# Batch row 0 of a gated linear attention prepared in three tiles of 128 rows, with its first pieces loaded through ScalarE's queue

## The chip, the core and the metric

The kernel runs on one core of a Trainium2 chip. The metric is the device time of one execution in microseconds. The core has five engines with queues of their own: TensorE (PE; its weight loads are PEld in the profile), VectorE (DVE), ScalarE (ACT), GpSimd (POOL) and SyncE (SP), and 16 DMA engines that serve the DMA queues of SP, ScalarE and GpSimd. Within a queue instructions run in the order in which the program was written; engines wait for one another through semaphores.

## The reference

A gated linear attention over 4 batch rows of 8 heads, 768 positions and 48 features, and behind it two layers of experts. Only the attention is touched:

```python
def _attn_ref(q, k, v, alpha):
    B, H, S, D = q.shape            # 4, 8, 768, 48
    state = np.zeros((B, H, D, D))
    for t in range(S):
        state = alpha[:, :, t, :, None] * state + np.einsum('bhd,bhe->bhde', k[:, :, t], v[:, :, t])
        y[:, :, t] = np.einsum('bhd,bhde->bhe', q[:, :, t], state)
```

Its output, as 3072 tokens of 384 features, goes through a layer that sends each token to the one of eight experts with the largest logit (`relu(x @ w1[e]) @ w2[e]`, times the gate's weight), and then through a dense layer `silu(x @ w_in) @ w_out`.

## The kernel before

The attention works on 16 pairs of heads, four to a batch row: pair p is pair p % 4 of batch row p // 4. In a pair, one head's 48 features lie on partitions 0 to 47 and the other's on 64 to 111; partitions 48 to 63 are a gap, and a pair fills 112 rows. A sequence is cut in six chunks of 128 positions.

Before PE can use a pair, its alpha, q and k have to be prepared: a running product of alpha (`f0`, line 535, a scan on DVE, with a reciprocal at line 538), q times that product (`scaled_q`, line 547; on GpSimd, but on DVE for tile 0), the decay of each chunk (`decay`, line 542, ScalarE), a scan from the end (`f1`, line 553, DVE) and k times that (`f2`, line 558, DVE). This runs on tiles T. In batch row 0 a tile is a pair: four tiles of 112 rows. In the batch rows 1 to 3 the fourth pair rides along with the other three: its 96 rows lie in six blocks of 16 in the gaps and behind the ends of three tiles, which so have 128 rows (`ASIDE`). When the three are prepared, six DMAs of 16 rows, issued by GpSimd, collect the fourth pair (`gather_last`, line 520). The prepared tiles are `Es[0]` to `Es[4]`, taken in turn and called E_133 to E_137 in listings; the collected pair is `Es[5]`, E_138. The profile calls them all E.

The loop over p from 0 to 16 (a step) does pair p's scores (`scores`, line 580, PE), transposes of k (`ks_transpose`, 568), the chunk updates (`updates`, 613 and 620) and the state scan (`states`, 630 on DVE, 647 on ScalarE), and beside them the output of pair p - 1 (`from_states`, 658, and `within`, 670 and 673). The masks on the scores are DVE's (586); for the first half of pairs 1 to 4 ScalarE copies and GpSimd masks (599 and 600). The steps of the preparation are hung into the loop by the table `work`: with place(T) = (b, j) and p = 4b + j, the first scan, q's multiply and the decay of tile T come in step p - 2, the reverse scan at the end of step p - 2, k's multiply at the head of step p - 1, and the loads at the start of step p - 3. Tiles 0 to 2 are loaded ahead of the loop. v comes in four buffers, three steps ahead (line 448). Small matmuls on zeros (`warm`, line 508) fill PE in the first steps. At step 2 GpSimd also makes constants.

Everything is issued in the order in which it is written (`manual_schedule`). All loads are SP's, one `dma_start` at a time, and eight such DMAs share eight semaphores in turn: an issue waits until the DMA that used the same one before has landed. All score matmuls write one pair of PSUM banks, so pair p + 1's scores wait for the masks of pair p.

## Time and profile before

| | |
|---|---|
| median of 3 runs | 794.62 us (793.44 to 795.41) |
| the profiled execution | 795.29 us |
| its span | 793.6 us |
| mean granted clock of TensorE | 0.991 |
| PE busy | 768.1 us, 97% |
| DVE busy | 478.9 us, 60% |
| DMA traffic | 80.54 MB, mean 101 GB/s |

The span runs from the first to the last instruction; the execution's own time has 1.7 us more around it. The attention lies in the first 160 us, the experts behind it. Busy time is a share of an average: DVE is at nine tenths in the first stretches of the page and at three or four behind 400 us.

### The profile page before, as it was taken

The page shows a single profiled execution, that of the slowest core. Times are in us where ns is not written, and L with a number is a line of the kernel's source. Part 1 is how long each engine was busy: PE and PEld are TensorE (multiplying, and loading weights), DVE is VectorE, ACT ScalarE, POOL GpSimd, SP SyncE. Part 2 cuts the span into 40 slices and gives each one's busy share as a digit, 9 for nine tenths or more (in the row PEclk, how much of TensorE's full clock was granted, in tenths as well). Part 3 has the DMA queues.
Part 4 walks back from the last instruction along what each step waited for, and adds up shares of the span by engine and source line. Part 5 has one row for each costly group of instructions (what it writes and reads, how often), then busy time and mean ns, then how long its engine had stood idle before and what let it go on. Part 6 is the DMA issues. An engine that isn't in the chain of part 4 may idle for free.

```text
span 793.6 us, 13367 instructions
## 1 busy us (share of the span) xinstructions
PE 768.1 (97%) x5104; PEld 701.0 (88%) x5104; DVE 478.9 (60%) x821; ACT 360.8 (45%) x685; POOL 156.5 (20%) x198
## 2 busy tenths in 40 slices
PE   8999998989999999999999999999999999999995
PEld 6878787889899999999999999999999998999985
DVE  8999975747787887788788433433443343333332
ACT  2656564425444455556544324453544444333322
POOL 4764321230332231311121200020020001002002
PEclk9999999999999999999999999999999999999998
DMA  9788883524554555555210110031022001001001
GB/s 241 212 197 223 217 251 96 172 80 124 172 170 145 183 193 160 189 179 164 94 63 18 38 55 18 0 93 36 1 75 52 19 1 40 2 0 41 1 1 44
DMA packets 41642, 80.54 MB, mean 101 GB/s; under 512 B 5640, under 2 KB 19863, under 8 KB 41568
## 3 DMA queue, kind: packets, MB, share of 16 engines
q1 hardware_dynamic: 37568, 67.56, 29.1%
q0 software_dynamic: 4000, 12.03, 5.1%
q8 instruction: 42, 0.69, 0.4%
q14 instruction: 32, 0.26, 0.1%
HBM read 68.03 MB, written 9.44 MB: 98 GB/s over the span
## 4 chain that ended last, share of the span: by engine, by line
issue 42%; PE 40%; DMA 5%; DVE 4%; POOL 4%; SPq 2%; ACT 2%; POOLq 0%; DVEq 0%; ACTq 0%
PE hp L1197 17%; PE both L1226 9%; PE yb L1226 4%; POOL out_dram L1415 3%; PE both L1393 1%; PE ob L1393 1%; SPq L439 1%; DMA E<-in_q_dram 1%; DMA E<-in_k_dram 1%; PE Yp L658 1%; DMA v__342<-in_v_dram 1%; PE xt L356 1%; PE Yp L673 1%; PE Ap L580 1%; DVE Pf L535 1%
## 5 line engine op out<-in xcount | busy, mean ns | idle before, releaser
L1197 PE MATMUL hp<-xh,wl 128*128 128x512 f32 (+9 forms) x504 | 184.5, 369 | 0.8 <-DVE wl L332 0.8
L1197 PE MATMUL hp<-xh,wh 128*128 128x512 f32 (+9 forms) x504 | 184.5, 369 | 0.0
L1371 DVE TENSOR_TENSOR sg<-hp,sg 128x512 f32<-128x512 f32 (+1 forms) x97 | 66.5, 686 | 157.6 <-ACT sg L1370 153.2
L1197 PE MATMUL hp<-xl,wh 128*128 128x512 f32 (+9 forms) x504 | 130.7, 367 | 0.0
L1370 ACT ACTIVATE sg<-hp 128x512 f32<-128x512 f32 (+1 forms) x97 | 57.5, 593 | 154.8 <-PE hp L1197 149.4
L1197 PEld LDWEIGHTS hp<-xh,wl 128*128 128x128 f32 x504 | 95.3, 189 | 10.1 <-DVE wl L332 0.9
L1197 PEld LDWEIGHTS hp<-xh,wh 128*128 128x128 f32 x504 | 95.1, 189 | 9.9 <-issue 0.4
L1197 PEld LDWEIGHTS hp<-xl,wh 128*128 128x128 f32 x504 | 91.9, 189 | 13.4
L1381 DVE TENSOR_TENSOR hl<-sg,hh 128x512 fp32r<-128x512 f32 x94 | 65.1, 692 | 61.1 <-PE ob L1393 40.5
L1380 ACT CAST hh<-sg 128x512 fp32r<-128x512 f32 x94 | 58.3, 620 | 70.3 <-DVE sg L1371 70.3
L1206 ACT ACTIVATE hh<-hp 128x192 fp32r<-128x192 f32 (+8 forms) x72 | 34.5, 479 | 117.6 <-PE hp L1197 113.4
L1415 POOL DMA_INDIRECT out_dram<-o,sidx x24 | 24.2, 1008 | 322.3 <-ACT o L1413 317.8
L1124 POOL TENSOR_TENSOR wl<-dx,wh 128x384 fp32r<-128x384 f32 x32 | 39.1, 1221 | 194.9 <-ACT wh L1121 191.3
L332 DVE TENSOR_TENSOR wl<-raw,wh 128x768 fp32r<-128x768 f32 x64 | 62.1, 971 | 11.1 <-ACT wh L331 9.9
L1393 PE MATMUL both<-wh,hh 128*128 128x384 f32 x188 | 64.1, 341 | 0.0
L1393 PE MATMUL both<-wh,hl 128*128 128x384 f32 x188 | 64.0, 341 | 0.0
L1208 DVE SCALAR_TENSOR_TENSOR hl<-hp,hh 128x192 fp32r<-128x192 f32 (+8 forms) x72 | 38.9, 540 | 41.2 <-ACT hh L1206 39.9
L1393 PE MATMUL both<-wl,hh 128*128 128x384 f32 x188 | 63.5, 338 | 0.0
L1393 PE MATMUL ob<-wh,hh 128*128 128x384 f32 x188 | 62.8, 334 | 0.0
L1393 PE MATMUL ob<-wl,hh 128*128 128x384 f32 x188 | 62.8, 334 | 0.0
L1393 PE MATMUL ob<-wh,hl 128*128 128x384 f32 x188 | 62.8, 334 | 0.0
L331 ACT CAST wh<-raw 128x768 fp32r<-128x768 f32 x64 | 52.9, 828 | 0.0
(363 smaller groups left out, 1482.2 us busy)
## 6 DMA issues: line engine op xcount, KB each, us to landing
raw<-in_wt_dram SPq DMA_DIRECT2D x64, 384.0 KB, 3.1
raw<-in_w_dram SPq DMA_DIRECT2D x32, 384.0 KB, 3.0
raw<-in_alpha_dram SPq DMA_DIRECT2D x16, 336.0 KB, 3.5
x_d<-xr SPq DMA_DIRECT2D x24, 192.0 KB, 1.9
E<-in_q_dram SPq DMA_DIRECT2D x18, 144.0 KB, 3.9
E<-in_k_dram SPq DMA_DIRECT2D x18, 144.0 KB, 2.8
E<-E POOLq DMA_DIRECT2D x18, 114.0 KB, 5.3
E<-in_q_dram SPq DMA_DIRECT2D x4, 336.0 KB, 9.3
```

The source lines that it names most:

```text
L331: nc.scalar.copy(hi, raw[t])
L332: eng.tensor_tensor(lo, raw.pop(t), hi.bitcast(F32), op=ALU.subtract)
L1124: nc.gpsimd.tensor_tensor(r["lo"], r["x"], r["hi"].bitcast(F32), op=ALU.subtract)
L1197: nc.tensor.matmul(hp, lhsT=a[:, kc * 128 : (kc + 1) * 128], rhs=x[:, kc, c0:c1], start=(i == 0), stop=(i == 8))
L1208: nc.vector.scalar_tensor_tensor(hl[:, :n], in0=hp, scalar=0.0, in1=hh[:, :n].bitcast(F32), op0=ALU.max, op1=ALU.subtract)
L1226: nc.tensor.matmul(yb[dc][:, c0:c1], lhsT=a[:, c : c + 128], rhs=b_[:, : c1 - c0], start=(f == 0 and i == 0), stop=(f == NF - 1 and i == 2),)
L1370: nc.scalar.activation(sg[:, z], hp[:, z], AF.Sigmoid)
L1371: nc.vector.tensor_tensor(sg[:, z], hp[:, z], sg[:, z], op=ALU.mult)
L1380: nc.scalar.copy(hh[:, z], sg[:, z])
L1381: nc.vector.tensor_tensor(hl[:, z], sg[:, z], hh[:, z].bitcast(F32), op=ALU.subtract)
L1393: nc.tensor.matmul(yb[tt], lhsT=a[:, tt * 128 : (tt + 1) * 128], rhs=b_[:, 384:768], start=(f == 0 and i == 0), stop=(f == NF2 - 1 and i = ...
L1415: sc = nc.gpsimd.indirect_dma_start(out=out, out_offset=bass.IndirectOffsetOnAxis(ap=sidx[:, i : i + 1], axis=0), in_=ob, in_offset=None,)
```

## The change

Batch row 0 is prepared as the others are: three tiles of 128 rows, with its fourth pair in their spare rows, and `gather_last(0)` in step 1 collects it. There are 12 tiles instead of 13. A tile's load is four DMAs for each of alpha, q and k, where batch row 0 had one: two of 48 rows and two of 16. The pieces of 16 now go first; those of tile 0 are issued by ScalarE's queue, all others by SP. Tile 0's alpha is still loaded in two halves of its columns, which makes four pieces of 48 rows. On DVE the reverse scan of tile 0 now stands ahead of its multiply by q.

```diff
--- before.py
+++ after.py
@@ -393,7 +393,7 @@
 
 
         ASIDE = (((0, 16), (0, 32)), ((1, 0), (1, 16)), ((1, 32), (0, 0)))
-        NTL = 4 + 3 * (B - 1)
+        NTL = 3 * B
         NE = 5
 
 
@@ -401,10 +401,7 @@
         tl = {}
 
         def place(T):
-            if T < 4:
-                return 0, T
-            b, j = divmod(T - 4, 3)
-            return b + 1, j
+            return divmod(T, 3)
 
         def parts(e):
             return dict(
@@ -429,18 +426,15 @@
             for x in what:
                 src, t = load_to(T, x)
                 n = src.shape[2]
-                z = src[4 * b + j]
-                if b:
-                    z = [(0, z[0:D]), (64, z[64:PA])]
-                    for i, (h, d) in enumerate(ASIDE[j]):
-                        s0 = 64 * h + d
-                        z.append((64 * i + D, src[4 * b + 3][s0 : s0 + 16]))
-                    for r0, y in z:
-                        nc.sync.dma_start(t[r0 : r0 + y.shape[0]], y)
-                else:
-
-                    for c0, c1 in ((0, SP // 2), (SP // 2, n)) if x == "a" and T == 0 else ((0, n),):
-                        nc.sync.dma_start(t[0:PA, c0:c1], z[:, c0:c1])
+                z = [(64 * h, src[4 * b + j][64 * h : 64 * h + D]) for h in range(2)]
+                for i, (h, d) in enumerate(ASIDE[j]):
+                    s0 = 64 * h + d
+                    z.append((64 * i + D, src[4 * b + 3][s0 : s0 + 16]))
+                for r0, y in z[2:]:
+                    (nc.sync if T else nc.scalar).dma_start(t[r0 : r0 + 16], y)
+                for c0, c1 in ((0, SP // 2), (SP // 2, n)) if x == "a" and T == 0 else ((0, n),):
+                    for r0, y in z[:2]:
+                        nc.sync.dma_start(t[r0 : r0 + D, c0:c1], y[:, c0:c1])
 
         def load_v(p):
             if p < NP:
@@ -517,17 +511,17 @@
             for j in range(3):
                 for i, (h, d) in enumerate(ASIDE[j]):
                     s0 = 64 * h + d
-                    nc.gpsimd.dma_start(Es[NE][s0 : s0 + 16], Es[(3 * b + 1 + j) % NE][64 * i + D : 64 * i + 64])
+                    nc.gpsimd.dma_start(Es[NE][s0 : s0 + 16], Es[(3 * b + j) % NE][64 * i + D : 64 * i + 64])
 
         def begin(p):
             b, j = divmod(p, 4)
-            e = Es[p if not b else NE if j == 3 else (3 * b + 1 + j) % NE]
+            e = Es[NE if j == 3 else (3 * b + j) % NE]
             st.setdefault(p, {}).update(parts(e))
 
         def prep(T):
             s = tl[T]
             i = T % 2
-            n = PA if T < 4 else 128
+            n = 128
 
             def f0():
                 s["Pf"] = wk.tile([128, SP], F32, tag="Pf", name="Pf", bufs=3)
@@ -1002,7 +996,7 @@
             for T, i in work.get((p, place), []):
                 f(T, i)
 
-        for i in range(5):
+        for i in (P_SCAN, DECAY, R_SCAN, Q_SCALE, K_SCALE):
             f(0, i)
         for i in (P_SCAN, Q_SCALE, DECAY):
             f(1, i)
@@ -1024,7 +1018,7 @@
                 ks_transpose(p, 0, 3)
                 if beside_scans(p, 0):
                     mask_aside(p, 0)
-            if p % 4 == 1 and 1 < p < NP:
+            if p % 4 == 1 and p < NP:
                 gather_last(p // 4)
             prepare(p, "scan")
             aside(p, "F1")
```

The order of the instructions is that of the code. On GpSimd, this stood ahead of the constants before (E_134 to E_137 are the tiles 1 to 4, Pf the scan's result, Am the masked scores; line 547 is q's multiply, line 600 the mask):

```order
L547 TENSOR_TENSOR E_2_135<-E_2_135,Pf_278 112x768
L600 AFFINE_SELECT Am_364<-Am_364 128x768
L547 TENSOR_TENSOR E_3_136<-E_3_136,Pf_374 112x768
L600 AFFINE_SELECT Am_458<-Am_458 128x768
L547 TENSOR_TENSOR E_4_137<-E_4_137,Pf_468 128x768
L478 MEMSET bm_89 112x1
```

And this stands there now (E_138 is the collected pair; lines are six lower):

```order
L541 TENSOR_TENSOR E_2_135<-E_2_135,Pf_302 128x768
L594 AFFINE_SELECT Am_388<-Am_388 128x768
L514 DMA E_5_138<-E_0_133 16x1824 x2
L514 DMA E_5_138<-E_1_134 16x1824 x2
L514 DMA E_5_138<-E_2_135 16x1824 x2
L594 AFFINE_SELECT Am_481<-Am_481 128x768
L541 TENSOR_TENSOR E_3_136<-E_3_136,Pf_490 128x768
L472 MEMSET bm_89 112x1
```

The multiply of pair 3's own tile has gone, the six DMAs stand between the masks of pair 1 and pair 2, and tile 3, which is pair 4's now, comes ahead of the constants, as pair 4's did.

On DVE, steps 1 and 2 before (So is the state scan, Rv the reverse scan, mask the mask's multiply):

```order
L558 TENSOR_TENSOR E_2_135<-E_2_135,Rv_340 112x768
L535 SCALAR_TENSOR_TENSOR Pf_374<-a__254,Z1_158 112x774
L538 RECIPROCAL D1_1_162<-Pf_374 112x6
L586 TENSOR_TENSOR Am_400<-Ap_393,mask_165 128x768
L630 SCALAR_TENSOR_TENSOR So_424<-U_179,E_1_134 112x288
L553 SCALAR_TENSOR_TENSOR Rv_431<-a__254,D1_1_162 112x774
L558 TENSOR_TENSOR E_3_136<-E_3_136,Rv_431 112x768
L535 SCALAR_TENSOR_TENSOR Pf_468<-a__344,Z1_158 128x774
L538 RECIPROCAL D1_0_161<-Pf_468 128x6
L586 TENSOR_TENSOR Am_521<-Ap_514,mask_165 128x768
L630 SCALAR_TENSOR_TENSOR So_545<-U_179,E_2_135 112x288
```

And now:

```order
L552 TENSOR_TENSOR E_2_135<-E_2_135,Rv_364 128x768
L580 TENSOR_TENSOR Am_425<-Ap_418,mask_193 128x768
L624 SCALAR_TENSOR_TENSOR So_449<-U_207,E_1_134 112x288
L529 SCALAR_TENSOR_TENSOR Pf_490<-a__368,Z1_186 128x774
L532 RECIPROCAL D1_1_190<-Pf_490 128x6
L580 TENSOR_TENSOR Am_543<-Ap_536,mask_193 128x768
L624 SCALAR_TENSOR_TENSOR So_567<-U_207,E_2_135 112x288
```

A scan and a reciprocal have left step 1, and the reverse scan and k's multiply between the two state scans have gone with them; the rest keeps its order.

On PE, pair 3's first scores read the collected pair, and their waits are now these (DMASW0 to DMASW5 are the six DMAs of GpSimd):

```order
L574 MATMUL Ap_593<-E_5_138 128x128 [waits DMASW1_49,DMASW5_49,DMASW0_49,DVE_49]
L574 MATMUL Ap_593<-E_5_138 128x128 [waits DMASW4_49,DMASW3_49,DMASW2_49]
L574 MATMUL Ap_593<-E_5_138 128x128 x4
L562 MATMUL Tp_602<-ident_78,E_5_138 128x112 x3
L502 LDWEIGHTS wz_76
```

The matmuls themselves stand where they stood; what they wait for has moved from a tile of SP's loads to the six DMAs.

## Rows read from the trace of the kernel before

**Rows 1.** The page, part 1: busy us (share of the span) and instructions.

```profile
PE 768.1 (97%) x5104; PEld 701.0 (88%) x5104; DVE 478.9 (60%) x821; ACT 360.8 (45%) x685; POOL 156.5 (20%) x198
```

**Rows 2.** Windows: stretch, its length, busy us by engine, PEclk, DMA share, GB/s.

```profile
9.60:18.40 8.80, 6.62 (x79) 5.33 (x79) 8.63 (x10) 1.92 (x4) 4.77 (x4) 1.00 1.06 262
...
25.00:31.50 6.50, 6.42 (x92) 5.34 (x89) 6.43 (x7) 4.12 (x8) 4.06 (x3) 1.00 0.58 166
...
31.50:38.00 6.50, 6.35 (x91) 5.33 (x89) 6.43 (x7) 4.03 (x8) 6.04 (x25) 1.00 0.83 230
...
164.00:793.00 629.00, 620.71 (x3273) 574.72 (x3272) 344.52 (x600) 278.59 (x516) 90.54 (x102) 0.99 0.25 76
```

**Rows 3.** Timeline of PE: start us, length us, engine, line, operation [idle before].

```profile
25.15 0.94 PE L580 MATMUL Ap<-E 48*128 48x128 f32 x12
...
31.58 0.94 PE L580 MATMUL Ap<-E 48*128 48x128 f32 x12
...
33.90 0.41 PE L568 MATMUL Tp<-ident,E 112*128 112x112 f32 x2 [0.15 <-ACT kst L571]
...
38.11 0.94 PE L580 MATMUL Ap<-E 48*128 48x128 f32 x12
...
45.79 1.03 PE L580 MATMUL Ap<-E 48*128 48x128 f32 x12 [1.38 <-POOL Am L600]
```

**Rows 4.** Timeline of DVE: tile 3's work, then a stretched scan and a mask.

```profile
21.64 1.76 DVE L535 TENSOR_TENSOR_SCAN Pf<-a__254,Z 112x774 f32<-112x774 f32 x1
...
25.04 2.25 DVE L553 TENSOR_TENSOR_SCAN Rv<-a__254,D 112x774 f32<-112x774 f32 x1
...
27.32 0.96 DVE L558 TENSOR_TENSOR E<-E,Rv 112x768 f32<-112x768 f32 x1
...
41.42 3.20 DVE L535 TENSOR_TENSOR_SCAN Pf<-a__558,Z 128x774 f32<-128x774 f32 x1
...
44.76 0.93 DVE L586 TENSOR_TENSOR Am<-Ap,mask 128x768 f32<-128x768 f32 x1
```

**Rows 5.** Timeline of GpSimd (POOL): two operations, then the first gather's six DMA issues.

```profile
21.66 2.40 POOL L600 TENSOR_SCALAR_AFFINE_SELECT Am<-Am 128x768 f32<-128x768 f32 x1 [2.56 <-ACT Am L599]
...
40.66 2.33 POOL L547 TENSOR_TENSOR E<-E,Pf 128x768 f32<-128x768 f32 x1
...
46.83 2.24 POOL L520 DMA_DIRECT2D E<-E  x4
...
50.88 0.96 POOL L520 DMA_DIRECT2D E<-E  x2 [1.82 <-DMA E<-in_q_dram]
```

**Rows 6.** Line 520's own view, its 18 gather DMAs: last line of it.

```profile
DMA to landing us min/median/max: 4.1/5.3/7.9
```

**Rows 7.** Timeline of DVE, the start of the kernel.

```profile
3.40 1.82 DVE L535 TENSOR_TENSOR_SCAN Pf<-a__139,Z 112x387 f32<-112x387 f32 x2 [1.01 <-DMA a__139<-in_alpha_dram]
...
6.00 0.96 DVE L547 TENSOR_TENSOR E<-E,Pf 112x768 f32<-112x768 f32 x1 [0.48 <-DMA E<-in_q_dram]
...
9.55 1.76 DVE L535 TENSOR_TENSOR_SCAN Pf<-a__144,Z 112x774 f32<-112x774 f32 x1
```

**Rows 8.** Timeline of SP's queue: the first DMA issues.

```profile
0.81 0.86 SPq L443 DMA_DIRECT2D a__139<-in_alpha_dram  x2
1.73 0.42 SPq L443 DMA_DIRECT2D E<-in_q_dram  x1
```

**Rows 9.** The page, part 6: DMA issues, count, KB each, median us to landing.

```profile
E<-in_q_dram SPq DMA_DIRECT2D x18, 144.0 KB, 3.9
E<-in_k_dram SPq DMA_DIRECT2D x18, 144.0 KB, 2.8
```

**Rows 10.** Timeline of PE at a wait, and windows of the stretches behind it.

```profile
130.53 0.69 PE L658 MATMUL Yp<-E,Sb 112*112 112x128 f32 x4 [2.42 <-ACT xb L690]
...
130.00:133.40 3.40, 2.87 (x22) 2.62 (x24) 1.78 (x2) 2.32 (x5) 0.00 (x0) 0.69 0.02 5
...
133.40:136.80 3.40, 3.40 (x38) 2.48 (x37) 1.43 (x4) 1.18 (x3) 0.00 (x0) 0.81 0.72 231
```

## The prediction

> **What bounds the kernel now.** I read the page first: PE is busy 97% of the span, DVE 60% [rows 1]. By stretches, everything from 164 us on is PE alone (620.71 of 629.00 us busy) [rows 2], and that work is not touched. What the attention gives or takes ahead of 164 us therefore reaches the end one for one, unless it moves something that waits on a clock of its own. So the question is what sets the pace in the first 46 us, where the change lies. A "step" p is one round of the loop, counted from the first score matmul (line 580) of pair p.
>
> The stretches show two engines close to full: in 9.6 to 18.4 us DVE (8.63 of 8.80 us, PE 6.62), and in the steps 2 and 3 both (PE 6.42 and 6.35 of 6.50 us, DVE 6.43 in each) [rows 2]. The timeline of PE settles which one a saving has to reach: pair 2's scores start at 25.15, pair 3's at 31.58, pair 4's at 38.11, with no idle time written beside these starts and 0.15 us in between at 33.90. The steps last 6.43 and 6.53 us, and PE fills them. PE's first real wait is ahead of pair 5's scores at 45.79, 1.38 us [rows 3]. The row puts it down to a GpSimd mask, but DVE's mask multiply, which started at 44.76 and took 0.93, ends at 45.69 [rows 4] on the score banks that these matmuls write: PE waits there for DVE.
>
> **The change, part by part.**
>
> *DVE loses one tile.* Pair 3 no longer has a tile of its own. Gone are a scan (1.76 us at 21.64), a reverse scan (2.25 at 25.04) and a multiply (0.96 at 27.32) [rows 4], with a reciprocal of 0.1 to 0.2: some 5.1 us. GpSimd loses one multiply of about 1.6 us, ScalarE one small activation; neither ends a wait there. As the order shows, the DVE work goes from steps 1 and 2. PE has no idle time there that DVE ends, so of the 5.1 us only what PE waits for later can be had: the 1.38 us at 45.79 and the 0.15 at 33.90 [rows 3]. Credit: 1.53 us. Its cover is DVE being early at step 4. DVE must not lose that lead again to GpSimd: the scan at 41.42 took 3.20 us, not 1.76 [rows 4], while GpSimd's multiply of 2.33 us at 40.66 ran [rows 5]. Both queues move by about the same amount, so I leave that stretch as it was; without the cover the credit falls towards 0.15.
>
> *A gather is added in step 1.* Pair 3's operands now come out of the spare rows of tiles 0 to 2 by six DMAs that GpSimd issues. They stand behind the mask of pair 1 (21.66 plus 2.40 us, so 24.06). Six issues took 2.24 + 0.96 = 3.20 us for batch row 1 [rows 5], so the last starts at about 26.8 us. The data they wait for (the multiply of tile 2 on DVE) is there by then, as it is ahead of the rows at 21.64. From issue to landing, such a DMA took 4.1, 5.3 and 7.9 us where the trace tells it [rows 6]. The last one lands at 30.9, 32.1 or 34.7. The reader of it is PE: pair 3's first two score matmuls wait for all six, and PE is ready for them at 31.58 [rows 3]. So the wait is between 0 and 3.1 us. I take 6.6 us, halfway between the two longer rows, because here the six are issued without the pause that the rows show between the fourth and the fifth (46.83, then 50.88 [rows 5]), so they queue behind each other: landing at 33.4, a wait of 1.8 us. Queued behind the six issues on GpSimd are pair 2's mask, pair 4's multiply and the constants; the mask and the multiply are read a step later, so I cost that at nothing. Without this cover it is at most the 3.2 us of issuing, less the 1.6 of the multiply removed.
>
> The Trainium skill (DMA: Bandwidth & Descriptors, section Anatomy of one DMA — SWDGE (gpsimd) path) fits one such transfer by about 2.0 us plus bytes at 436 GB/s, which for 114 KB is an estimate of 2.3 us. The trace does not agree: its shortest is 4.1 us [rows 6]. By the page, the last would land at 29.1, no wait would be left, and the sum would be that of the second rival below.
>
> *The start.* The alpha of tile 0 comes as two pieces of 48 rows by each half on SP and two of 16 on ScalarE's queue. An SP issue takes 0.43 us (0.86 for two, and the third follows 0.92 after the first [rows 8]): 0.46 with the gap. The first scan started at 3.40, behind the first issue [rows 7]; it now needs the second one too: +0.46. Ahead of the multiply by q DVE waited 0.48 us (at 6.00 [rows 7]); the reverse scan now goes first, and q has 1.8 us more: -0.48. These cancel, and tile 1's scan could start at 9.5 as before (9.55 [rows 7]). Its alpha, however, is SP's 9th to 12th issue and no longer its fifth. At 0.46 us each the last starts at 5.9; if the eight that may be in flight (an issue waits for the eighth ahead of it, by the order) each take 3.9 us [rows 9], the cadence is 0.49 and it starts at 6.2. It lands 2.8 to 3.9 us later [rows 9]: 8.7 to 10.1. So the start costs between 0 and 0.6 us; I take 0.2, as the middle of the landing lies at 9.4. ScalarE's issues are in no row; I price them as SP's, and its table load and first activation behind them are read only in step 0's last scan, 8 us later. The bytes add up to less than before (three tiles of 128 rows for four of 112).
>
> The Trainium skill (same page, section Rules for kernel authors) speaks against this part: transfers to separate groups of partitions go to the same 16 engines, one transfer is better, and spreading over issuing engines saves issue time alone. By it the start would sit at its upper bound, 0.6, and the sum at 795.5. The trace's rows for the small pieces [rows 9] leave both open.
>
> *Sum.* 0.2 (start) + 1.8 (gather) - 1.53 (PE's waits that go) = **+0.5 us**. The profiled execution took 795.29 us with a span of 793.6; it lies 0.67 above the median of the three timed runs (794.62). So 795.8 for its like, and **795.1 us** for the median. Of the unknowns, the gather runs from 0 to 3.1, the start from 0 to 0.6, the credit from 0.15 to 1.53: all of them at one end or the other give 793.1 and 798.2; with the credit whole and the gather late by 1 to 3 us it is 794.1 to 796.7.
>
> **Rivals.**
>
> *The gather is in time.* It needs the last DMA to land within 4.8 us of its issue. The shortest row (4.1) speaks for it, the median and the longest (5.3, 7.9) against it [rows 6]. Then 0.2 - 1.53 = -1.3: 793.3 us.
>
> *DVE was the bound after all.* If PE's full steps are full because it runs filler (the matmuls on zeros of line 508 stand in each of steps 1 to 4) and because the records end late, all 5.1 us come through: 789.5 us. DVE's 6.43 of 6.50 [rows 2] speaks for it, PE's rows with no idle time [rows 3] against it.
>
> *The loads starve DVE in the first 20 us (slower).* Tiles 0 to 2 now take 32 issues on SP and six on ScalarE where 10 did. If each of the three alphas comes late by 0.8 us, a little over the bound above, the start costs 2.4 instead of 0.2: 797.3 us. It decides for slower from a start of about 2.1 us. For it: DVE is full in 9.6 to 18.4 [rows 2], so nothing absorbs it. Against it: DMA moved 262 GB/s there [rows 2], and the bytes get fewer.
>
> *PE's clock falls.* Behind a wait of PE of 2.42 us that ended at 130.53 the granted clock is 0.69 in 130.0 to 133.4 and 0.81 in 133.4 to 136.8 [rows 10], the level of 1.2 GHz for part of both: 0.31 and 0.19 of 3.4 us each, 1.7 us of work. If the wait for the gather does the same in step 3, the sum grows by that, to 796.8 us.
>
> **How the numbers follow.** A time of this kernel tells a difference of about 0.3%, 2.4 us, from none. Forecast (gather late by 1 to 3 us): 0.44. Gather in time: 0.22. Clock falls: 0.14. Loads starve DVE: 0.12. DVE bound: 0.08. Faster than 792.2 is the DVE case alone, 0.08. Slower than 797.0 are 0.07 of the loads, 0.06 of the clock and 0.01 of a very late gather, 0.14. Same: 0.78. The range 793.0 to 797.6 leaves out the DVE case and the upper parts of the two slow ones.
>
> **What would show it.** In the changed kernel's PE timeline: idle time of 1 to 3 us ahead of pair 3's first score (released by a GpSimd DMA), then steps 3 and 4 with no wait of over 0.5 us ahead of pair 5's scores, which start within 1.5 us of 45.79. On DVE: the first scan at about 3.9, tile 1's at 9.5 to 10.1, idle time in steps 1 and 2. On GpSimd: six DMAs from about 24 us on. The forecast is wrong if pair 3's scores start without a wait, if DVE idles by more than 1 us in all for loads ahead of 20 us, if PE idles in step 2 instead of being full, or if something behind 46 us changes its length by more than 1 us.

## The result and the profile after

The changed kernel took 798.72 us (median of six runs, 798.41 to 801.66), the kernel before beside it 794.03; the ratio is 1.0059, with a 95% interval of 1.0032 to 1.0085. The forecast was 795.1, with a range up to 797.6: the change is slower, and by more than any of the cases that were given a chance. The profile shown here is that of the run of 801.66 us, the slowest of the six, whose span is 799.4; a second profile of the same kernel comes with the first experiment. One execution among the experiments below took 2656.32 us (the kernel before with row 0's loads cut); the ratio given there is that of the other eight.

First the page, part 1, of the changed kernel: busy us, share and instructions.

```profile
PE 772.5 (97%) x5104; PEld 704.3 (88%) x5104; DVE 471.7 (59%) x817; ACT 360.3 (45%) x684; POOL 151.4 (19%) x203
```

DVE has lost 7.2 us of work against [rows 1], more than the 5.1 that the forecast took away, and PE has as many instructions as it had. The time must have gone into waits or into PE's clock. The stretches (length, busy us by engine, PE's clock, DMA share, GB/s) show both:

```profile
9.60:18.40 8.80, 7.48 (x88) 5.91 (x85) 7.79 (x7) 1.30 (x3) 3.85 (x3) 1.00 0.81 216
18.40:25.00 6.60, 5.27 (x40) 4.87 (x42) 4.57 (x6) 3.36 (x6) 3.75 (x4) 0.74 0.93 258
20.70:24.20 3.50, 3.50 (x19) 3.33 (x18) 2.31 (x2) 2.42 (x5) 1.32 (x2) 0.51 1.00 274
```

In 9.6 to 18.4 us DVE was full before (8.63 of 8.80) and DMA moved 262 GB/s [rows 2]; now DVE works 7.79 and DMA moves 216. Less arrives, though less is in the way. From 20.7 on PE's granted clock is 0.51 for 3.5 us, the level of 1.2 GHz. DVE's timeline (start, length) says what it waited for:

```profile
4.14 1.82 DVE L529 TENSOR_TENSOR_SCAN Pf<-a__139,Z 128x387 f32<-128x387 f32 x2 [1.75 <-DMA a__139<-in_alpha_dram]
...
9.71 1.77 DVE L529 TENSOR_TENSOR_SCAN Pf<-a__154,Z 128x774 f32<-128x774 f32 x1
...
16.80 1.77 DVE L529 TENSOR_TENSOR_SCAN Pf<-a__169,Z 128x774 f32<-128x774 f32 x1 [0.87 <-DMA a__169<-in_alpha_dram]
```

The first scan starts 0.74 us later than in [rows 7], tile 1's (9.71) where the forecast had it, and tile 2's waits 0.87 us for an alpha that before was there long ahead. SP's queue shows why: the first of tile 2's four pieces of alpha is issued at 11.43 us and the last at about 12.8, where before its one DMA was issued at 4.56. First the two rows of the changed kernel, then SP's issue, DVE's scan and pair 1's scores before:

```profile
11.43 0.88 SPq L434 DMA_DIRECT2D a__169<-in_alpha_dram  x2
12.36 0.88 SPq L437 DMA_DIRECT2D a__169<-in_alpha_dram  x2
```

```profile
4.56 0.81 SPq L443 DMA_DIRECT2D a__150<-in_alpha_dram  x1
...
15.57 1.76 DVE L535 TENSOR_TENSOR_SCAN Pf<-a__150,Z 112x774 f32<-112x774 f32 x1
...
18.50 0.94 PE L580 MATMUL Ap<-E 48*128 48x128 f32 x12 [0.91 <-issue]
```

On PE, the starts of the scores of pairs 1, 2, 3 and 5:

```profile
19.73 0.47 PE L574 MATMUL Ap<-E 48*128 48x128 f32 x3 [1.96 <-issue]
...
27.61 0.94 PE L574 MATMUL Ap<-E 48*128 48x128 f32 x12
...
34.91 1.03 PE L574 MATMUL Ap<-E 48*128 48x128 f32 x12 [1.07 <-DVE Rv L547]
...
48.28 0.92 PE L574 MATMUL Ap<-E 48*128 48x128 f32 x11 [1.30 <-issue]
```

Pair 1's scores wait 1.96 us, 1.05 more than before, and start 1.23 later; behind that wait the clock falls, and pair 2's are 2.46 late against [rows 3]. Pair 3's wait 1.07 us more (the row names DVE's reverse scan of tile 3, which pair 3 does not read; the mask multiply that its scores need from DVE ended at 32.51, so the six gather DMAs are left, and the second profile names them). At pair 5 the kernel is 2.49 us behind, where the forecast had it 0.5 behind. The rest of the 5.8 us of span comes later, with falls of the clock in 102.7 to 106.1 and 136.8 to 143.6. The kernel before had two there too in its profile (3.4 us each, from 131.3 and 162.0), so the changed one has 3.4 us more of the lower level between 50 and 170 us, some 1.7 us of work. The other five runs took 1.7 to 3.3 us less.

### The profile page after: what moved, and what is told of

It is laid out like the page before. It is cut to its first block, busy times and chain, and to the rows that moved or that the text cites. A ratio compares the mean times of both kernels' runs of the same rounds, so it can differ in the third digit from the quotient of the medians.

```text
span 799.4 us, 13417 instructions
## 1 busy us (share of the span) xinstructions
PE 772.5 (97%) x5104; PEld 704.3 (88%) x5104; DVE 471.7 (59%) x817; ACT 360.3 (45%) x684; POOL 151.4 (19%) x203
## 4 chain that ended last, share of the span: by engine, by line
issue 42%; PE 40%; DMA 7%; POOL 3%; DVE 3%; SPq 3%; ACT 1%; POOLq 0%; DVEq 0%; ACTq 0%
PE hp L1191 16%; PE both L1220 9%; PE yb L1220 4%; POOL out_dram L1409 3%; PE Ap L574 1%; PE Yp L652 1%; PE both L1387 1%; PE ob L1387 1%; PE xt L356 1%; DMA E<-in_q_dram 1%; DMA x_d<-xr 1%; SPq L437 1%; DMA a__1178<-in_alpha_dram 1%; DMA xg<-x_d,gidx 1%; PE Yp L667 1%
```

## Experiments

All numbers of time are ratios to the kernel before on the same chip, with 95% intervals. The table gathers what the sections below come back to: when pair 1's, 3's and 5's scores start in the profile of each run, and where PE's clock was at its lower level ahead of 50 us.

| kernel | ratio | pair 1 | pair 3 | pair 5 | lower clock from (us long) |
|---|---|---|---|---|---|
| before | 1 | 18.50 | 31.58 | 45.79 | - |
| changed | 1.0059 | 19.73 | 34.91 | 48.28 | 20.75 (3.4) |
| changed, again | 1.0045 (1.0028 to 1.0062) | 19.51 | 35.05 | 48.60 | 35.67 (3.4) |
| before + six copies | 1.0025 (1.0009 to 1.0040) | 18.47 | 33.32 | 48.17 | 34.39 (3.4) |
| before, row 0's loads cut | 1.0056 (1.0035 to 1.0077) | 19.91 | 35.14 | 50.09 | - |
| gather earlier | 1.0048 (1.0030 to 1.0067) | 20.62 | 36.51 | 49.58 | 22.42 (6.8) |
| one DMA per operand | 0.9962 (0.9946 to 0.9978) | 17.90 | 30.71 | 43.78 | - |
| no gather | 1.0024 (1.0007 to 1.0042) | 20.59 | 36.54 | 49.61 | 22.49 (6.8) |
| one DMA, no gather | 0.9972 (0.9957 to 0.9987) | 17.91 | 30.73 | 43.80 | - |
| one DMA, gather by ScalarE | 0.9995 (0.9975 to 1.0015) | 17.85 | 32.50 | 45.58 | - |
| one DMA for row 0 only | 0.9986 (0.9969 to 1.0003) | 17.89 | 30.71 | 43.82 | - |
| before, one DMA for rows 1 to 3 | 0.9977 (0.9962 to 0.9992) | 18.81 | 32.66 | 46.36 | - |
| pieces on two queues | 1.0084 (1.0062 to 1.0105) | 28.44 | 40.73 | 53.81 | 14.35 (13.7) |
| all pieces on SP | 1.0064 (1.0043 to 1.0085) | 22.11 | 38.01 | 51.56 | 16.01, 39.90 (3.4 each) |
| two even pieces | 1.0036 (1.0016 to 1.0056) | 23.34 | 35.63 | 48.70 | 12.75 (10.2) |
| four even pieces | 1.0056 (1.0035 to 1.0078) | 21.06 | 35.28 | 48.86 | 14.97 (3.4) |
| more filler | 1.0027 (1.0005 to 1.0049) | 21.24 | 34.84 | 47.44 | - |
| one DMA per operand, again | 0.9975 (0.9960 to 0.9990) | 17.93 | 30.75 | 43.82 | - |
| before, one DMA for rows 1 to 3, again | 0.9980 (0.9969 to 0.9991) | 18.58 | 31.67 | 45.88 | - |
| one DMA per operand, adds moved | 0.9931 (0.9910 to 0.9951) | 17.86 | 30.68 | 43.75 | - |

**Which half of the change costs: the loads or the gather?** The four runs of this question ran side by side. First the changed kernel once more, with no edit.

> The changed kernel itself, unchanged, profiled again: its first profile was of its slowest execution (801.66 us, with two stretches of PE at the lower clock that the others may not have). Loads theory (the pieces of the split tiles come late on DVE in the first 20 us, and all that follows is late by it): pair 1's scores start 1 to 1.3 us later than before's 18.50, pair 2's 1.2 to 2.5 later than 25.15. Gather theory (the six copies come late themselves and hold up the loads of the tiles behind them): pair 3's scores wait about 1 us and start 0.9 us or more further behind than pair 2's, and pair 5's scores do not win back the 1.5 us. Clock theory (it is a chance fall of PE's clock): with the clock full in the first 30 us, pair 6's scores start within 1 us of before's 53.64. All theories: the time is 798 to 800.

The ratio is 1.0045. Both theories find what they named in this profile: pair 1 is 1.01 us late, and pair 3's scores wait 2.67 us. The third, a chance fall of the clock, does not hold alone: the clock is full up to 35.67, and pair 6's scores still start at 56.19, 2.55 us late. The chain of work that ended last, followed back from pair 3's scores (start us, length, what), holds both:

```profile
12.29 0.42 SPq L437
...
12.76 3.70 DMA a__169<-in_alpha_dram
...
16.58 1.78 DVE Pf L529
...
22.65 1.41 POOL Am L594
24.06 0.20 POOL E L514
...
24.75 1.92 POOL E L514 x4
26.67 8.24 DMA E<-E
```

SP issues piece behind piece up to 12.7 us, tile 2's alpha takes 3.70 us to land, the work on DVE, ScalarE and GpSimd follows without a gap, and the last of the six copies, issued at 26.67, lands 8.24 us later at 34.91. PE was ready at 32.38.

Next the kernel before with copies that nobody reads, and the kernel before with the loads cut:

```diff
+            if p == 1:
+                for s0 in (16, 32, 64, 80, 96, 0):
+                    r0 = 48 if s0 % 32 else 96
+                    nc.gpsimd.dma_start(Es[NE][s0 : s0 + 16], Es[2][r0 : r0 + 16])
```

> The kernel before, with six copies of 16 rows that nobody reads added on GpSimd's queue in step 1, where the changed kernel has its gather; the copies are extra work. Gather theory: they hold up the loads and the masks behind them, DVE waits for a tile's alpha in step 2 to 4, and the time is 1 to 3 us longer than before (795.0 to 797.0). Loads theory: 0 to 0.5 us (794.0 to 794.6), with pairs 1 and 2 where they were and pair 5's scores within 0.5 us of 45.79.

```diff
+                    for r0 in (48, 64):
+                        (nc.sync if T else nc.scalar).dma_start(t[r0 : r0 + 16], z[r0 : r0 + 16])
                     for c0, c1 in ((0, SP // 2), (SP // 2, n)) if x == "a" and T == 0 else ((0, n),):
-                        nc.sync.dma_start(t[0:PA, c0:c1], z[:, c0:c1])
+                        for r0, r1 in ((0, 48), (80, PA)):
+                            nc.sync.dma_start(t[r0:r1, c0:c1], z[r0:r1, c0:c1])
```

> The kernel before, with the loads of batch row 0 alone cut as the changed kernel cuts them (pieces of 16 rows, tile 0's through ScalarE's queue, and two larger ones); the same bytes, four tiles as before, no gather. Loads theory: DVE waits for alpha at tile 0 (0.7 us) and tile 2 (0.9 us), pair 1's scores start about 1.2 us late, pair 2's 1.2 to 2.5, and the time is 1.2 to 3 us longer than before (795.2 to 797.0). Gather theory: 0 to 0.5 us (794.0 to 794.5). If loads and gather each take a part, this run and the one with the gather alone add up to the changed kernel's 4.7 us and the credit that it should have had, 6.2 us.

The copies alone cost 2.0 us (0.25%), the cut alone 4.4 (0.56%, above the 3 that was expected). So the cut alone gives at least the changed kernel's whole loss; the copies' price in the kernel before is real too, but it comes by another way than their waiting. GpSimd's multiply stands behind the six issues and now falls on DVE's multiply by k, which takes 3.65 us instead of the 0.96 of [rows 4]:

```profile
26.82 3.65 DVE L558 TENSOR_TENSOR E<-E,Rv 112x768 f32<-112x768 f32 x1
```

```profile
27.17 1.67 POOL L547 TENSOR_TENSOR E<-E,Pf 112x768 f32<-112x768 f32 x1
28.76 0.89 POOL L600 TENSOR_SCALAR_AFFINE_SELECT Am<-Am 128x768 f32<-128x768 f32 x1
```

GpSimd's mask stands right behind its multiply and ends at 29.65; DVE's multiply ends 0.82 us behind it. The next scan and pair 2's mask multiply come some 2.2 us later than before, the mask ends at 33.22 and not at 31.03, and pair 3's scores, which write the same banks, wait 1.66 us and start at 33.32.

In the changed kernel that multiply of GpSimd's and that one of DVE's are gone, so this price can't be added to the other. The two sum to 6.4 us, where the changed kernel's loss on this chip and the forecast's credit make 5.1 (3.6 + 1.5); the difference lies within the intervals, and the sums weren't bound to agree.

```diff
-        def gather_last(b):
+        def gather_last(b, js=range(3)):
...
             prepare(p, "head")
+            if p == 0:
+                gather_last(0, (0, 1))
...
-                gather_last(p // 4)
+                gather_last(p // 4, (2,) if p == 1 else range(3))
```

> The changed kernel with the copies of tiles 0 and 1 issued a step earlier, so that step 1 issues only tile 2's two. Gather theory: the last copy lands about 2 us earlier, pair 3's scores no longer wait (1.07 us before), the loads behind it run undisturbed, and the time is 1 to 2.5 us shorter than the changed kernel's (796.2 to 797.7). Loads theory: the first two steps are as late as they were, and the copies in step 0 now stand beside tile 2's loads: the same as the changed kernel, or up to 1 us longer (798.7 to 799.7).

1.0048, as the loads theory had it: pair 3's scores no longer wait, but pair 1's are 2.12 us late and the clock falls for 6.8 us. The four copies in step 0 run among tile 2's loads; DVE waited 2.12 us for tile 2's k.

**Loads and gather, each taken away.** In the next four, again side by side, "one DMA" means that the inputs are stored in the tiles' order ahead of the kernel:

```diff
-                for r0, y in z[2:]:
-                    (nc.sync if T else nc.scalar).dma_start(t[r0 : r0 + 16], y)
+                z = {"a": at_, "q": qt, "k": kt}[x][T]
...
-                    for r0, y in z[:2]:
-                        nc.sync.dma_start(t[r0 : r0 + D, c0:c1], y[:, c0:c1])
+                    nc.sync.dma_start(t[:, c0:c1], z[:, c0:c1])
```

> The changed kernel with the operands of each tile stored beforehand in the tile's own order of rows, so that each of alpha, q and k is one DMA of 128 rows (tile 0's alpha in two halves by columns) and ScalarE's queue issues none; a pure rearrangement of the inputs ahead of the kernel. The gather stays. Loads theory: SP issues 3 or 4 DMAs a tile instead of 12, DVE no longer waits for the alpha of tiles 0, 2, 4 and 5 nor for k of tile 2, pair 1's scores start within 0.3 us of before's 18.50 and pair 2's within 0.3 of 25.15, and the time is 2 to 3.5 us shorter than the changed kernel's: against before between 0 and +1.8 us. Gather theory: pair 3's scores still wait 1 us or more for the last copy, and the time is 0 to 1.5 us shorter than the changed kernel's. Both: what is left over before is the wait for the copies less the credit that the forecast gave.

```diff
-            e = Es[NE if j == 3 else (3 * b + j) % NE]
+            e = Es[2 if p == 3 else NE if j == 3 else (3 * b + j) % NE]
...
-            if p % 4 == 1 and p < NP:
+            if p % 4 == 1 and 1 < p < NP:
```

> The changed kernel without batch row 0's gather: the six copies are left out and pair 3 reads tile 2 in the place of the gathered one, so that this part of the output is another. The split loads stay. Gather theory: pair 3's scores follow pair 2's without a wait, tile 4's and 5's alpha come in time for DVE, and the time is 2 to 4 us shorter than the changed kernel's. Loads theory: pair 1's scores stay 1 to 1.4 us late, pair 5's scores 1 to 2.5 us late, and the time is 0.5 to 1.5 us shorter than the changed kernel's (only the wait for the copies goes).

> Both together: one DMA per operand, and batch row 0's gather left out with pair 3 reading tile 2 (that part of the output is another). This is what the saving on DVE is worth with neither price. If the forecast's credit was right, pair 5's scores start about 1.5 us ahead of before's 45.79 and the time is 1.3 to 1.6 us shorter than before's. If DVE was the bound after all, it is 3 to 5 us shorter. If the credit was never there (something else is late at pair 5, such as a multiply of DVE's that GpSimd's work stretches), it is within 0.5 us of before.

With one DMA per operand the ratio is 0.9962, 3 us shorter than before and some 6.6 shorter than the changed kernel: more than was expected. Leaving the gather out as well changes nothing that can be measured (0.9972, and the same starts within 0.02 us). Leaving it out while the loads stay cut gives 1.0024; the starts show no gain there (pair 5 at 49.61), since the clock fell in that profile for 6.8 us; the ratio's interval overlaps that of the changed kernel, measured on another chip. So the gather costs nothing that can be measured when the loads are whole; what it costs beside cut loads is told by the waits of 1.07 and 2.67 us at pair 3, not by this run.

The kernel with one DMA per operand, its stretches, SP's issue of tile 2's alpha, and PE at pairs 3 and 5:

```profile
0.00:9.60 9.60, 8.46 (x60) 6.72 (x62) 7.30 (x11) 1.91 (x2) 3.58 (x16) 1.00 0.79 273
9.60:18.40 8.80, 6.93 (x87) 5.66 (x87) 8.63 (x10) 1.92 (x4) 5.37 (x4) 1.00 0.98 378
18.40:25.00 6.60, 6.33 (x93) 5.25 (x92) 5.35 (x6) 4.04 (x8) 4.04 (x8) 1.00 0.23 42
```

```profile
5.07 0.90 SPq L434 DMA_DIRECT2D a__150<-in_at_dram  x1
```

```profile
30.71 0.72 PE L571 MATMUL Ap<-E 48*128 48x128 f32 x8
...
43.78 0.68 PE L571 MATMUL Ap<-E 48*128 48x128 f32 x7 [1.10 <-POOL Am L591]
```

The loads move at 378 GB/s instead of 216 and are through before 25 us. The six copies are issued from 21.88 to 25.0, 2.1 us earlier than in the changed kernel, since the mask ahead of them is earlier; in 18.4 to 25.0 DMA moves 42 GB/s, and 282 in 25.0 to 31.5. They land ahead of pair 3's scores, which start without a wait.

```diff
-            if p % 4 == 1 and p < NP:
+            if p % 4 == 1 and 1 < p < NP:
...
                 ks_transpose(p, 3, 5)
+                if p == 1:
+                    gather_last(0, nc.scalar)
```

> As the run with one DMA per operand, with batch row 0's six copies issued on ScalarE's queue, late in step 1 behind its copy of the transposed keys, instead of on GpSimd's. If the wait for the copies lies in GpSimd's kind of queue, the last lands 2 to 3 us after its issue at about 26, pair 3's scores start without a wait, and the time is 1 to 2 us shorter than with GpSimd's copies: 0 to 1.5 us shorter than before. If it lies in the DMA engines being full of loads, the last lands 4 us or more after its issue and the time is within 0.5 us of that with GpSimd's copies; ScalarE's copies of the outputs behind the six issues come up to 1 us late in either case.

0.9995: 2.6 us longer than with GpSimd's copies. With whole loads no wait for the copies was left that another queue could shorten, so the run tells nothing on GpSimd's queue against full DMA engines. It shows that ScalarE has no room for six issues: they hold it from 20.83 to 25.64, and the second half of pair 2's scores starts at 29.30 instead of 27.51.

**Which loads, and what of them?** The next four ran side by side.

> The changed kernel with one DMA of 128 rows per operand for batch row 0's three tiles alone (tile 0's alpha in two halves by columns); the tiles of rows 1 to 3 load in four pieces as in the kernel before. The inputs for row 0 are rearranged ahead of the kernel, nothing else. If the cutting of row 0's loads is what made the change slow, pair 1's scores start at about 17.9 and pair 5's at 43.8, as with all tiles in one DMA, and the time is 1 to 3 us shorter than before's. If the gain of the run with all tiles in one DMA came from rows 1 to 3, this one is within 1 us of the changed kernel, 2.5 to 4.5 us longer than before's.

> The kernel before (four tiles of 112 rows for batch row 0) with one DMA per operand for the tiles of rows 1 to 3, rearranged ahead of the kernel. If row 0's loads are the whole cause, this is within 0.8 us of before, pair 5's scores within 0.3 us of 45.79. If the four pieces of the later tiles cost time too (their alpha late for DVE behind 46 us), it is 1 to 3 us shorter than before's.

```diff
+                if T < 3:
+                    z = {"a": at_, "q": qt, "k": kt}[x][T]
+                    for c0, c1 in ((0, SP // 2), (SP // 2, n)) if x == "a" and T == 0 else ((0, n),):
+                        nc.sync.dma_start(t[:, c0:c1], z[:, c0:c1])
+                    continue
```

(for the first; the second has the one DMA in the branch of `b`). With row 0's tiles alone in one DMA, the ratio is 0.9986 and pair 5 starts at 43.82: the cutting of row 0's loads is the whole difference between the changed kernel and one that is as fast as before (1.1 us shorter, with an interval that reaches 1). The kernel before gains 1.8 us when rows 1 to 3 load in one DMA; that it stands later at pair 5 (46.36) shows that this gain lies behind 46 us.

```diff
-                    (nc.sync if T else nc.scalar).dma_start(t[r0 : r0 + 16], y)
+                    (nc.sync if T > 2 else nc.scalar).dma_start(t[r0 : r0 + 16], y)
```

> The changed kernel with the pieces of 16 rows of all three tiles of batch row 0 issued through ScalarE's queue, 18 of them ahead of its table load, and only the pieces of 48 rows on SP: as many pieces, half as many issues on SP. If the time of an issue on SP (0.46 us each, one after the other) makes tile 2's operands late, its alpha and k come in time, pair 1's scores start within 0.5 us of 18.50, and the time is 2 to 5 us shorter than the changed kernel's. If it is the pieces themselves on the DMA engines, tile 2's alpha lands as late as it did, and the time is within 1 us of the changed kernel's.

1.0084, and neither reading fits: tile 2's alpha did come in time (its scan starts at 16.20 with no wait), but ScalarE is held by its own issues. Its timeline:

```profile
15.38 0.97 ACTq L434 DMA_DIRECT2D E<-in_k_dram  x2
16.38 1.28 ACT L536 ACT_TABLE_LOAD   x1 [16.38 <-DMA E<-in_q_dram]
...
18.69 0.42 ACT L565 COPY kst<-Tp 128x336 f32<-128x336 f32 x1
```

The copy of the transposed keys, at 12.32 in the changed kernel's second profile, comes at 18.69; PE waits and runs 13.7 us at the lower clock. The run tells nothing on issues against transfers.

> The changed kernel with tile 0's six pieces of 16 rows on SP as all others, so that ScalarE's queue issues no DMA. Part of the time lies outside the span: 1.73 us in before and in the runs with one DMA per operand, 1.98 to 2.17 in those whose ScalarE issues loads. If that comes with the second queue, it is 1.73 here. Inside the span all issues of SP come later by six times 0.46 us: the first scan starts at 4.9 to 5.2 and tile 2's alpha comes 2 us later than in the changed kernel; the time is 1 to 4 us longer than the changed kernel's. If the pieces' transfers and not SP's issues are the limit, it is within 1 us.

1.0064, some 1.5 us above the changed kernel (on another chip, and the intervals overlap). The profile is as it should be if SP's issues are the limit: the first scan starts at 4.35 (not as late as expected), tile 2's alpha is issued from 13.3 on, pair 1's scores start at 22.11, and pair 3's after a wait of 3.02 us for the copies.

**The number of DMAs or their shape?** Two runs cut row 0's whole DMAs by rows, from the source in order (the edit is shown for four pieces, against the run with one DMA per operand for row 0; for two, `R` is `(0, 64, 128)` throughout); the third is the changed kernel with `warm(44)` for `warm(22)`.

```diff
-                        nc.sync.dma_start(t[:, c0:c1], z[:, c0:c1])
+                        R = (0, 48, 96, 128) if c1 < n or c0 else (0, 32, 64, 96, 128)
+                        for r0, r1 in zip(R, R[1:]):
+                            nc.sync.dma_start(t[r0:r1, c0:c1], z[r0:r1, c0:c1])
```

> As the run with batch row 0 in one DMA per operand, with each of those DMAs cut in two of 64 rows (the same rearranged source, all on SP). If the number of DMAs is what makes the operands late, tile 2's alpha and k are issued some 3 us later than with one each, but still ahead of their readers: pair 1's scores within 0.4 us of 17.9, and the time 0 to 1 us longer than with one DMA per operand (ratio to before 0.998 to 1.000). If the pieces' size and place matter and not their number, the same as with one DMA.

> The same with four pieces of 32 rows per operand, six for tile 0's alpha: as many DMAs as in the run with all pieces on SP (1.0064 of before), of even size and from a source in order. If the number counts, it is as slow as that run within 1.5 us: ratio 1.005 to 1.008, the first scan at 4.9 or later, pair 1's scores at 20 or later. If the pieces of 16 rows and their scattered sources are the cause, it stays near the run with one DMA per operand, 0.998 to 1.001.

Four even pieces cost as much as the changed kernel's uneven ones: 1.0056, though the first scan started at 3.79 and not at 4.9. Tile 2's scan starts at 18.13, behind a wait of 0.83 us for its alpha. The number counts, not the 16 rows or the scattered source. SP's queue and the stretches of that run:

```profile
3.56 1.82 SPq L437 DMA_DIRECT2D E<-in_qt_dram  x4
5.42 1.82 SPq L437 DMA_DIRECT2D E<-in_kt_dram  x4
7.28 1.81 SPq L437 DMA_DIRECT2D a__154<-in_at_dram  x4
```

```profile
0.00:9.60 9.60, 8.24 (x58) 6.48 (x58) 6.55 (x10) 1.91 (x2) 3.58 (x16) 1.00 0.53 153
9.60:18.40 8.80, 6.21 (x62) 5.03 (x63) 6.66 (x7) 1.30 (x3) 3.85 (x3) 0.81 0.75 208
```

Four issues take 1.86 us from start to start, 0.465 each, with no gap; the DMA engines are half idle (0.53). SP is the limit. Two pieces were expected to cost at most 1 us over one and cost 4.0 (1.0036 against 0.9986, each beside its own runs of the kernel before). Each issue took 0.62 us there (the DMAs of v, with 128 rows, 0.58), so DVE waited 0.46 us for tile 0's k and 0.59 for tile 1's alpha; tile 2's alpha, issued at 10.22, was there when its scan started at 17.20. Most of the loss at pair 1 is the clock's: PE ran at the lower level from 12.75 to 23.0, the 22 filler matmuls that take 2.58 us before took 4.59, and pair 1's scores, for which DVE's mask was done at 20.02, started at 23.34. So this run does not price the number of pieces by itself. Why issues were slower in it is open.

> The changed kernel with 44 instead of 22 matmuls on zeros in step 0, ahead of PE's wait for pair 1; it computes the same. If falls of PE's clock behind that wait are part of the loss, no stretch at the lower clock begins between 16 and 30 us, and the time is 0.7 to 2 us shorter than the changed kernel's (which was 1.0045 of before, 3.6 us): ratio 1.002 to 1.0035. If the clock plays no part, the time is that of the changed kernel, 1.0045, or up to 1 us longer for the added matmuls.

1.0027, with no fall ahead of 50 us, and a granted clock of 0.9945 on average over the runs (before beside it 0.9942), where the changed kernel had 0.9925 (before beside it 0.9951). So some 1.4 of the changed kernel's 3.6 us hang on the clock, within intervals that overlap and on two chips. The clocks say much the same: the changed kernel's is 0.0026 below that of the kernel before beside it, and of 792 us that share is 2.1, an estimate.

**Is the forecast's credit there when the loads are whole?** The two kernels with one DMA per operand, side by side:

> The changed kernel with one DMA per operand for all tiles, now beside the kernel before with the same loads. If the saving on DVE is worth what pair 5's scores showed, this one is 1.3 to 2.6 us shorter than the other; if DVE was the bound, 4 us or more; if the two are within 0.8 us, the change gives nothing even with whole loads.

> The kernel before with one DMA per operand for the tiles of rows 1 to 3, beside the changed one with the same loads: 0.5 to 2.5 us shorter than before's, and 1.3 to 2.6 us longer than the changed one with whole loads if the credit is there.

They take the same time: 789.29 and 789.36 us (0.9975 and 0.9980). Yet pair 5's scores start at 43.82 in the one and at 45.88 in the other. So 2.06 us are won at pair 5 and lost again behind it. The starts on PE tell where: 1.30 us are left at 58.34 against 59.64, 0.6 from 66 to 154 us, and at 157.78 against 157.27 the changed one is 0.51 behind. In step 6 of the changed one, DVE and GpSimd:

```profile
55.82 1.60 DVE L773 TENSOR_TENSOR cb<-carry,e 128x8 f32<-128x8 f32 x1
57.35 0.94 DVE L577 TENSOR_TENSOR Am<-Ap,mask 128x768 f32<-128x768 f32 x1
```

```profile
55.77 1.63 POOL L538 TENSOR_TENSOR E<-E,Pf 128x768 f32<-128x768 f32 x1 [5.91 <-DVE Pf L526]
```

And in the other:

```profile
57.89 0.13 DVE L780 TENSOR_TENSOR cb<-carry,e 128x8 f32<-128x8 f32 x1
57.93 0.95 DVE L584 TENSOR_TENSOR Am<-Ap,mask 128x768 f32<-128x768 f32 x1
```

```profile
57.89 1.63 POOL L545 TENSOR_TENSOR E<-E,Pf 128x768 f32<-128x768 f32 x1 [5.97 <-PE Ap L578]
```

An add of 128x8 takes 1.60 us where GpSimd's multiply began 0.05 us ahead of it, and 0.13 where the two began together. The mask multiply behind it comes late, and PE waits 0.69 us at 58.34 and then 0.57 for ScalarE's copy of the states. The last 0.6 goes in this profile at the first experts' rows, at which PE waits 1.49 us in the changed one and 0.97 in the other:

```profile
157.78 0.47 PE L359 MATMUL xt<-ident,xg 64*128 64x64 f32 x2 [1.49 <-DMA xg<-x_d,gidx]
```

```profile
157.27 0.40 PE L359 MATMUL xt<-ident,xg 64*128 64x64 f32 x3 [0.97 <-DMA xg<-x_d,gidx]
```

The profile of the changed one is that of its slowest execution, 793.33 us, so that this holds for the others is not shown; over the runs its clock was also lower, 0.9948 against 0.9966.

The last run makes the small add a step of its own and puts it ahead of the scan. The line stands for batch rows 0 and 1, so it moves two adds, that of step 6 and that of step 10:

```diff
                 at |= {
+                    (p + 1, "A"): [s_["carried"]],
                     (p + 1, "F2"): [s_["ranks"]],
```

> The changed kernel with one DMA per operand, with batch row 0's small add (carried counts plus offsets) issued in step 6 ahead of the scan instead of behind it, where GpSimd's multiply begins at the same moment. If that add lost a race, the mask multiply behind the scan starts 0.9 to 1.5 us earlier, PE's wait of 0.69 us ahead of the second half of pair 6's... the scores that followed at 58.34 goes, pair 7's scores keep most of the 2 us, and the work up to 149 us stands 1.2 to 2 us ahead of the kernel before with whole loads instead of 0.62; of that the wait for the experts' rows at 158 may take all: the time is 0 to 1.3 us shorter than that of the run without the move, ratio 0.996 to 0.9975. If any work of DVE's is held beside GpSimd's multiply, the mask multiply takes 1.6 us longer in the add's place and nothing changes, ratio 0.9975.

0.9931, with an interval of 0.9910 to 0.9951: 5.5 us shorter than before, and the fastest of all. In step 6 the add and the mask multiply now stand so, with GpSimd's multiply at 55.79:

```profile
53.86 0.16 DVE L777 TENSOR_TENSOR cb<-carry,e 128x8 f32<-128x8 f32 x1
...
55.85 0.93 DVE L577 TENSOR_TENSOR Am<-Ap,mask 128x768 f32<-128x768 f32 x1
```

The lost race is shown as the cause of the wait in step 6: the mask multiply beside GpSimd's takes its 0.93 us, and the scores start at 57.53 instead of 58.34 and without a wait. The first experts' rows are read at 155.09, 2.18 us ahead of the kernel before with whole loads. Not all of that is the credit kept. The add of step 10 took 1.60 us, at 85.29 and 85.91, in both kernels with whole loads, and takes 0.15 at 81.88 here: ahead of it this run leads the changed one without the move by 1.50 us (scores at 83.30 against 84.80), behind it by 2.61 (89.68 against 92.29). Against the two runs without the move (0.9962 and 0.9975) the ratio is 2.5 to 3.5 us better, more than the 1.3 expected; the second add is 1.1 of it by these starts, they ran on other chips, and the clock was 0.9964 here against 0.9952 and 0.9948.

## Why the prediction was wrong

**The start: 0.2 us, bound 0.6. This step failed.** It followed the split loads to tile 0's and tile 1's alpha, and there it was right in the two profiles of the changed kernel (first scan 0.74 to 0.79 us late, the reverse scan first giving back what q's wait had cost, tile 1's scan at 9.7 to 10.0). It stopped one tile short. SP's issues go out one by one at 0.46 us, so tile 2's alpha, the ninth issue before, becomes SP's 22nd to 25th, from 11.4 us on instead of at 4.56. DVE waits 0.26 to 1.45 us for it in the five profiles with the changed kernel's loads, and starts tile 2's scan at 16.58 to 18.06 instead of 15.57. The argument against the rival was "DMA moved 262 GB/s there, and the bytes get fewer". Bytes were not the limit, and their rate does not tell how full the DMA engines are: 262 GB/s kept them 1.06 busy before, 378 GB/s 0.98 with whole DMAs of 128 rows, and in pieces they were 0.81 and 0.91 busy at 216 and 236. At pair 1 the start cost 1.0 and 1.2 us in the two profiles, and 2.1 in the two with the gather earlier or left out; its own sign of being wrong, DVE idle by over 1 us for loads ahead of 20, showed: 0.74 more than before at the first scan and 0.87 at tile 2's.

The Trainium skill (DMA: Bandwidth & Descriptors, section Rules for kernel authors) says that transfers to separate parts of the partitions gain nothing and that one of 128 partitions is to be used. The runs agree: one DMA per operand for row 0 gives 0.9986, two pieces 1.0036 (with the clock's part in it), four 1.0056. The forecast weighed that rule, found it worth 0.4 us more at most, and left it out of its sum; the rows that it held against it, [rows 9], are of pieces of 48 rows (144 KB), not of 16. The same section says that further issuing engines save issue time only; in this kernel issue time was the price itself.

**The gather: 1.8 us, bounds 0 to 3.1. The mechanism was right, the size inside the bounds.** The waits were 1.07 and 2.67 us. The longest landing was 8.24 us, above the longest row of before, 7.9 [rows 6]. What the step missed is that the landing hangs on the loads: with row 0 in one DMA each the copies cost nothing, the case of the rival "in time" (the first in the forecast's list, which it once calls the second). In the second profile the DMA engines were 0.96 busy in 21.9 to 25.0 and 1.04, at 173 GB/s, while the copy of 8.24 us was under way; with one DMA per operand they were 0.46 busy in 21.9 to 25.0, where the six are issued. That this queue at their issue makes the landing late is argued from these rows, not shown by a run. The loads behind the gather, which the sum left out, were late as well: SP needed 11 us for tile 4's twelve pieces from 28.3 on, and in the second profile DVE waited 2.52 us for that tile's alpha. No wait of PE's shows for it, since DVE's next mask then waited for PE's scores.

**The credit: 1.53 us. Right where it was looked for, and then not kept.** With whole loads pair 5's scores start 1.97 to 2.06 us ahead, 0.6 of it from the first tile's order of work (tile 1's scan starts at 8.95 instead of 9.55), and PE still waits 1.10 us there. In the changed kernel the second profile gives the sum in the forecast's own terms at pair 5: PE ready for pair 3 0.80 late, the copies 2.67, one fall of the clock 1.7, together 5.17; pair 5's scores are 2.81 late, so 2.36 were made good. The forecast had 0.2 + 1.8 - 1.53.

**"What the attention gives or takes … reaches the end one for one, unless it moves something that waits on a clock of its own." This failed for gains: they met the exception, for which the sum had no term.** Losses do go on, as far as the rows were followed: 2.81 us at pair 5 are 2.69 at 69.58 against 66.89. The gain of 2.06 us met two such waits, GpSimd's multiply in step 6 and, in one profile, the experts' rows. The Trainium skill (SBUF — State Buffer, section SBUF: two separate sides) says that VectorE and GpSimd share a pair of ports, which the one that starts first holds for its whole instruction when DVE's has two inputs in SBUF. The rows agree for the add (both inputs in SBUF; 1.60 us, its end just behind GpSimd's) and for the mask multiply, whose one input is in PSUM (0.93 us in the middle of GpSimd's 1.64). DVE's multiply of 3.65 us in the run with copies alone fits only with both of GpSimd's operations beside it counted, the multiply and the mask, and although DVE's row begins 0.35 us ahead of the first.

**The rivals.** "The loads starve DVE" (0.12) and "PE's clock falls" (0.14) were both true, and together: in most of these profiles the clock fell behind a wait that the late loads made. Each was priced alone (797.3, 796.8). In the profiles with row 0's loads in pieces the clock fell ahead of 50 us in eight of ten (not in the kernel before with the cut, nor in the one with more filler); in the ten with row 0's loads whole it fell once, behind the wait that the copies in the kernel before made. Taking the rivals as separate cases, and not as one that brings on the other, is why the range ended at 797.6. "DVE was the bound" did not show: with whole loads and no gather, 5.1 us less work on DVE gave 2.0 at pair 5.

What stays open: how much of the 4.7 us in the first measurement, against 3.6 on the second chip, is falls of the clock behind 50 us; where the last 0.6 us of the credit goes in a run of median time; and why some 0.3 us of the difference lie outside the span (before 1.73 us on average, the changed kernel 1.98 to 2.17, 1.70 with all pieces on SP, but 1.72 also with 18 pieces through ScalarE's queue).

## What to carry to other kernels

Count the DMAs ahead of each operand, not its bytes alone: on SP's queue, back to back, each issue took 0.46 to 0.47 us from start to start for 16, 32 and 48 rows, and the same for whole DMAs of 128 rows in the first 4 us; and look at the operand behind all the added issues, not only at the first. A saving on an engine that is ahead is worth nothing until the next thing with a clock of its own has been looked at; follow a gain through the stages behind it as one follows a loss. And where a wait and a fall of the clock can follow from each other, price them together.

## What the runs showed of the hardware

- An add of 128x8 on DVE took 1.60 us when GpSimd's multiply had begun 0.05 us earlier, and 0.13 when both began together; with two such adds moved out of the way the scores stood 2.61 us earlier at 90 us.
- With row 0's operands in one DMA each, 262 and 339 GB/s moved in 0 to 9.6 and 9.6 to 18.4 us, with the DMA engines 0.79 and 0.96 busy; in four pieces each, 153 and 208 GB/s, with 0.53 and 0.75.
- Issues on SP took 0.62 us each in the run with two pieces of 64 rows, and 0.465 in that with four of 32.
- A copy of 114 KB through GpSimd's queue landed after 8.24 us while the DMA engines were 1.04 busy at 173 GB/s. With whole loads all six, issued while the engines were 0.46 busy (21.9 to 25.0), were there when PE came for them at 30.71.
- DVE's multiply of 112x768 took 3.65 us instead of 0.96 while GpSimd ran a multiply and a mask from 27.17 to 29.65.
